# Sliding-window attention beside an MLP: the row maxima reach the q stacks through VectorE's 32x32 squares and transfers, not through a TensorE turn

## The chip, the cores and the metric

One core of a Trainium2 chip runs the whole program. The metric is the device time of one execution in microseconds (us). The kernel before takes 813.5 us (median of 3 runs, 813.16 to 815.95). TensorE (PE) multiplies, PEld is its loading of weights, VectorE is DVE, ScalarE is ACT, GpSimd is POOL, and SyncE (SP) issues every transfer.

## The reference, cut to what matters

```python
qkv = (x @ wqkv) -> q, k, v          # S = 2048 tokens, D = 512, H = 32 heads of 16
scores = q . k * 16 ** -0.5          # masked: 0 <= query - key < 256
p = softmax(scores)                  # over the keys
a = (p . v) @ wo
b = gelu(x @ w1 + b1) @ w2 + b2      # F = 1792
g = sigmoid(sum(x * gate_w))
out = g * a + (1 - g) * b
```

Everything is float32. The softmax is taken with the row maximum subtracted, so the maximum of each query's row has to be known before its exponentials.

## The kernel before, in words

Each dense product is made of three TensorE products of float32r halves (`mm3`, L100 to L103). The projections come first; then the attention and the MLP run interleaved, and the output projection (`final`) ends the program.

Attention goes through 8 groups of 4 heads, and in each group through 16 blocks of 128 tokens. A **step** `u` is one block of keys of one group; there are 128. In a step `att_exp` (L425) makes four score tiles `st` [128 keys x up to 384 queries] (L433), one for each head `i`; ACT takes their exponentials (L445), POOL cuts the edges of the window (L437, L440), and `att_pv` multiplies by v (L465). The exponentials need the maxima of the queries, and these are made by a second pass, `att_max` (L381): for the query block `LEAD` = 6 steps ahead, four tiles `sm` (L389) of the same scores, now with queries on the partitions, and DVE reduces each to its maximum (`M`, L394).

The maximum then has to lie along the columns of the query operand. The stack `qs` holds q for the four heads as 96 rows (high and low parts), and rows 96 and up are for the maxima; `ks` has ones (`own`) in the rows that belong to a head, so that the product `st` comes out with the maximum subtracted. All maxima are handled in **pairs** of blocks (`RB` = 2), 64 pairs in all. `att_rows` (L401) makes the negated maximum as a high and a low part on DVE (`nm`, L405 and L406; 16 columns: 2 blocks, 4 heads, 2 parts). `att_turn` (L410) turns it on TensorE with a product by the identity (L413, tile `mp` in the same three PSUM buffers as `sm`), and ACT writes the rows into `qs` twice (L418), once for each block of the pair, with a scale of 0 or 1 from `odd` that clears the rows of the other block. A pair's rows are first read by `st` two steps after the step that made the last of its maxima has ended.

A chunk of 4 blocks of q and k comes from DRAM for each next group (`att_load`, L353 and L354, every fourth step, when the max block's number leaves `LPOS` = 2 after division by 4); v comes in `att_load_v` (L376); the sums of a chunk go out (`ND`, L477) and are divided in `att_norm` (L500 to L512).

The order on PE, ACT, DVE and POOL is written out by the program: a clock of modelled nanoseconds (`tick`) advances with the products, and work is put in with `after(ns, ...)` when it falls due. Each step takes `STEP` = 2345 ns of dense work from the MLP (3150 ns, `STEP0`, in the first `LEAD` steps, which only make maxima). The order on SP is made by the scheduler from the dependencies. Each transfer has one of eight semaphores in turn, and waits until the transfer eight before it has landed.

Of the kernel before, what the change touches and what calls it, by code (L numbers as in the profile page):

```python
# [32 lines left out]
def gated_mix(ctx: ExitStack, tc: tile.TileContext, x, wqkv, wo, w1, b1, w2, b2, gate_w, out):  # L33
    nc = tc.nc
    x = x[0]
    out = out[0]

    cp = ctx.enter_context(tc.tile_pool(name="cp", bufs=1))
    sb = ctx.enter_context(tc.tile_pool(name="sb", bufs=1))
    dr = ctx.enter_context(tc.tile_pool(name="dr", bufs=1, space=DRAM))  # L40
    ps = ctx.enter_context(tc.tile_pool(name="ps", bufs=1, space=PSUM))
# [3 lines left out]
    def f32(ap):  # L45
        return ap.bitcast(F32)
# [16 lines left out]
    identr = cp.tile([128, 128], F32R, name="identr")  # L63
# [10 lines left out]
                            compare_op=ALU.is_ge, fill=NEG, base=-1, channel_multiplier=-1)  # L74
    nc.gpsimd.affine_select(out=mask[:, 256:384], in_=mask[:, 256:384], pattern=[[-1, 128]],
                            compare_op=ALU.is_ge, fill=NEG, base=0, channel_multiplier=1)


    own = cp.tile([128, 4], F32, name="own")
    nil = cp.tile([128, 1], F32, name="nil")  # L80
    nc.gpsimd.memset(nil, 0.0)
    nc.gpsimd.memset(own, 0.0)
    for k in (0, 1, 8, 9):
        nc.gpsimd.affine_select(out=own[96:112], in_=own[96:112], pattern=[[-2, 4]], compare_op=ALU.not_equal,
                                fill=1.0, base=-k, channel_multiplier=1)
    odd = cp.tile([128, 2], F32, name="odd")
    nc.gpsimd.memset(odd, 0.0)
    nc.gpsimd.memset(odd[96:104, 0:1], 1.0)
    nc.gpsimd.affine_select(out=odd[96:112, 1:2], in_=odd[96:112, 1:2], pattern=[[0, 1]], compare_op=ALU.is_ge,
                            fill=1.0, base=7, channel_multiplier=-1)  # L90
    nms = [cp.tile([128, 112], F32R, name=f"nm{i}") for i in range(2)]
    for nm in nms:
        nc.gpsimd.memset(f32(nm), 0.0)
    vbuf = cp.tile([128, 2, NB * 68 + 16], F32, name="vbuf")
# [83 lines left out]
    qs = cp.tile([128, 2, S], F32R, name="qs")  # L178
# [221 lines left out]
    def att_rows(g_, rb):  # L400

        need(*[("max", g_, rb * RB + b, i) for b in range(RB) for i in range(4)])
        m = Ms.pop((g_, rb))
        nm = nms[rb % 2][:, 96:112].rearrange("p (b i k) -> p k b i", b=RB, k=2)
        nc.vector.tensor_scalar(nm[:, 0], m, -1.0, None, op0=ALU.mult)  # L405
        nc.vector.scalar_tensor_tensor(nm[:, 1], m, -1.0, f32(nm[:, 0]), op0=ALU.mult, op1=ALU.subtract)  # L406
        done.add(("nm", g_, rb))

    def att_turn(g_, rb):

        need(("nm", g_, rb))
        p = ps.tile([112, 128], F32, tag="sm", bufs=3, name=f"mp{g_}_{rb}")
        nc.tensor.matmul(p, nms[rb % 2], identr, start=True, stop=True)  # L413

        def put():
            for b in range(RB):
                cols = slice((rb * RB + b) * 128, (rb * RB + b + 1) * 128)
                nc.scalar.activation(qs[96:112, :, cols], p[96:112].unsqueeze(1).broadcast_to([16, 2, 128]),  # L418
                    AF.Copy, scale=odd[96:112, b:b + 1])
            done.add(("rows", g_, rb))  # L420
        tick(67)
        after(100, put)

    def att_exp(g_, kb, i):

        pr, s = divmod(i, 2)
        w = min(384, S - kb * 128)
        if s == 0:
            pts[g_, kb, pr] = sb.tile([128, 2, 384], F32, tag="pt", bufs=11, name=f"pt{g_}_{kb}_{pr}")
        pt = pts[g_, kb, pr]  # L430
        need(*[("rows", g_, b) for b in range(kb // RB, (kb + w // 128 - 1) // RB + 1)])
        p = ps.tile([128, 384], F32, tag="st", bufs=2, name=f"st{g_}_{kb}_{i}")
        nc.tensor.matmul(p[:, :w], ks[:, pr, s, kb * 128:(kb + 1) * 128],  # L433
                         qs[:, pr, kb * 128:kb * 128 + w], start=True, stop=True)

        def sel():
            nc.gpsimd.affine_select(out=pt[:, :, 0:128], in_=pt[:, :, 0:128], pattern=[[0, 2], [1, 128]],  # L437
                                    compare_op=ALU.is_ge, fill=0.0, base=0, channel_multiplier=-1)
            if w == 384:
                nc.gpsimd.affine_select(out=pt[:, :, 256:384], in_=pt[:, :, 256:384], pattern=[[0, 2], [-1, 128]],  # L440
                                        compare_op=ALU.is_ge, fill=0.0, base=-1, channel_multiplier=1)
            done.add(("pt", g_, kb, pr))

        def exp():
            nc.scalar.activation(pt[:, s, :w], p[:, :w], AF.Exp, scale=SCALE)  # L445
            if s == 1:
                after(500, sel)
        tick(w / 2.4 + 13)
        after(100, exp)
# [257 lines left out]
    turn = None  # L707
    for u in range(-LEAD, NU):
        m = u + LEAD
        gm, bm = divmod(m, NKB)  # L710
        step = STEP if u >= 0 else STEP0
        for i in range(4):
            for op in ORDER:
                if op == "s" and u >= 0:
                    att_exp(u // NKB, u % NKB, i)
                if op == "m" and m < NU:
                    att_max(gm, bm, i ^ XOR)
                if op == "p" and i == PVAT and u >= 1:
                    att_pvs(u - 1)
                if op == "p" and i == PVAT and turn:  # L720
                    att_turn(*turn)
                    turn = None
                if op == "f":
                    fill(step / 4 / ORDER.count("f"))
        if m < NU and bm % RB == RB - 1:
            after(900, att_rows, gm, bm // RB)
            turn = (gm, bm // RB)
# [9 lines left out]

MANUAL = {mybir.EngineType.PE, mybir.EngineType.Activation, mybir.EngineType.DVE, mybir.EngineType.Pool}
MM3 = 3 * 227
LPOS = 2  # L740
LASTN = 2
YLAND = 3200
WARM = (7, 3)
RB = 2
NKB = S // 128
LEAD = 6
START = 117e3
NORM = 6000
GELU = (700, 1500, 2300, 3300, 4200, 5000)
# [5 lines left out]
AHEAD = 11e3  # L755
STEP0 = 3150.0
PVAT = 2
STEP = 2345.0
_TC = dict()
_INS = ["A_x", "A_wqkv", "A_wo", "B_w1", "B_b1", "B_w2", "B_b2", "gate_w"]  # L760

# [17 lines left out]
```

## Time and profile before

| | |
|---|---|
| median of 3 runs | 813.5 us |
| profiled execution, its time | 813.36 us |
| profiled execution, its span | 811.4 us |
| DVE busy | 513.7 us (63%) |
| ACT busy | 483.4 us (60%) |
| POOL busy | 338.7 us (42%) |
| L413, the turn, on PE: 64 | 19.8 us, mean 310 ns |
| L418, the rows written by ACT: 128 | 53.0 us, mean 460 ns |

The span runs from the first to the last instruction. Matmuls are pipelined, so the busy time of one overlaps that of the next: what a matmul takes from the engine is the time from its start to the next one's start, in the timeline, and not its own duration. An engine's idle time before an instruction is listed with what ended it. On SP only the issue of a transfer is seen, not its landing; a landing shows where something waits for it.

### The profile page before, as it was taken

The numbers are of one execution on the slowest core, as the hardware profiler recorded it, in microseconds if no ns is written. First come the engines' busy times: TensorE is split into PE (matmuls) and PEld (weight loads), VectorE is DVE, ScalarE is ACT, GpSimd is POOL, SyncE is SP. The second block draws the span as 40 slices with busy tenths as digits, with TensorE's granted clock in tenths as the row PEclk, the third lists the DMA queues.
The fourth block names the chain that finished last, engine by engine and source line by source line (L and its number), as shares of the span: only waits on it lengthen the run. The fifth ranks groups of instructions, "written<-read, shape, count | busy, mean of one in ns | idle before, by whom it ended". The sixth has DMA issues, their size and how long they took to land.

```text
span 811.4 us, 14841 instructions
## 1 busy us (share of the span) xinstructions
PE 788.5 (97%) x4694; PEld 616.6 (76%) x4694; DVE 513.7 (63%) x1517; ACT 483.4 (60%) x993; POOL 338.7 (42%) x611
## 2 busy tenths in 40 slices
PE   8999999999999999999999999999999999999998
PEld 6788888867877777688767867877777778777767
DVE  5433332887478758856885688568757865784353
ACT  4434423587568557755875677567656764876631
POOL 3200002396336425542784386336524552574100
PEclk9999999999999999999999999999999999999999
DMA  8985856536542734443234555542664363335873
GB/s 260 387 308 195 304 174 211 195 89 215 164 137 66 227 116 119 122 156 104 86 101 132 171 156 173 152 143 86 192 179 129 99 202 113 97 118 186 249 260 117
DMA packets 94925, 135.72 MB, mean 167 GB/s; under 512 B 32256, under 2 KB 43776, under 8 KB 94848
## 3 DMA queue, kind: packets, MB, share of 16 engines
q1 hardware_dynamic: 94848, 134.79, 52.3%
q8 instruction: 37, 0.61, 0.3%
q14 instruction: 40, 0.33, 0.1%
HBM read 79.70 MB, written 55.05 MB: 166 GB/s over the span
## 4 chain that ended last, share of the span: by engine, by line
PE 78%; DVE 8%; ACT 7%; DMA 2%; issue 2%; SPq 1%; POOL 1%; POOLq 0%; DVEq 0%; ACTq 0%
PE st L433 9%; PE pv L465 9%; PE sm L389 8%; PE y L101 6%; PE y L103 6%; PE y L102 6%; PE u L101 4%; PE u L102 4%; PE u L103 4%; PE qk L101 3%; PE qk L103 3%; PE qk L102 3%; DVE jm L394 2%; ACT pt L445 2%; PE v L103 2%
## 5 line engine op out<-in xcount | busy, mean ns | idle before, releaser
L394 DVE CUSTOM_DVE_ANT_0 jm<-sm,mask 128x384 bf16<-128x384 f32 (+2 forms) x512 | 270.6, 528 | 150.1 <-PE sm L389 128.7
L445 ACT ACTIVATE pt<-st 128x384 f32<-128x384 f32 (+2 forms) x512 | 231.0, 471 | 120.6 <-PE st L433 102.9
L437 POOL TENSOR_SCALAR_AFFINE_SELECT pt<-pt 128x256 f32<-128x256 f32 x256 | 122.3, 478 | 248.8 <-ACT pt L445 248.2
L433 PE MATMUL st<-qs,ks 128*128 128x384 f32 (+2 forms) x512 | 172.1, 338 | 8.1 <-ACT pt L445 7.1
L389 PE MATMUL sm<-ks,qs 96*128 96x384 f32 (+2 forms) x512 | 169.6, 332 | 1.8 <-DVE M L394 0.8
L433 PEld LDWEIGHTS st<-qs,ks 128*128 128x128 f32 x512 | 97.0, 190 | 37.1 <-ACT pt L445 19.4
L389 PEld LDWEIGHTS sm<-ks,qs 96*128 96x128 f32 x512 | 96.2, 188 | 26.0 <-DVE M L394 5.2
L440 POOL TENSOR_SCALAR_AFFINE_SELECT pt<-pt 128x256 f32<-128x256 f32 x224 | 101.9, 455 | 0.0
L465 PE MATMUL pv<-pt,vbuf 128*32 128x384 f32 (+2 forms) x1408 | 91.6, 389 | 0.1
L101 PE MATMUL y<-w,h 128*128 128x512 f32 x224 | 89.4, 399 | 0.0
L103 PE MATMUL y<-w,h 128*128 128x512 f32 x224 | 87.7, 391 | 1.3 <-POOL h L574 1.3
L102 PE MATMUL y<-w,h 128*128 128x512 f32 x224 | 87.7, 391 | 0.0
L574 POOL TENSOR_TENSOR h<-x1h,h 128x512 fp32r<-128x512 f32 x56 | 72.5, 1294 | 35.6 <-DVE h L571 35.2
L101 PE MATMUL u<-mx,w 128*128 128x512 f32 x196 | 79.3, 404 | 0.0
L102 PE MATMUL u<-mx,w 128*128 128x512 f32 x196 | 76.7, 391 | 0.0
L103 PE MATMUL u<-mx,w 128*128 128x512 f32 x196 | 76.6, 391 | 0.0
L418 ACT ACTIVATE qs<-mp,odd 16x256 fp32r<-16x256 f32 x128 | 53.0, 460 | 38.9 <-PE mp L413 37.9
L465 PEld LDWEIGHTS pv<-pt,vbuf 128*32 128x32 f32 x1408 | 38.5, 109 | 37.2 <-issue 24.2
L562 DVE SCALAR_TENSOR_TENSOR sqh<-sqh,x1h 128x512 f32<-128x512 f32 x56 | 51.6, 921 | 13.2 <-ACT sqh L559 13.2
L565 ACT ACTIVATE sqh<-sqh 128x512 f32<-128x512 f32 x56 | 35.5, 634 | 36.8 <-DVE sqh L562 36.2
L160 POOL TENSOR_TENSOR w<-raw_w,w 128x512 fp32r<-128x512 f32 x28 | 38.4, 1370 | 40.3 <-ACT w L156 40.2
L256 DVE TENSOR_TENSOR qke<-qk,qke 128x512 fp32r<-128x512 f32 x32 | 22.1, 691 | 51.3 <-ACT qke L253 49.6
(122 smaller groups left out, 1247.7 us busy)
## 6 DMA issues: line engine op xcount, KB each, us to landing
mx<-XT SPq DMA_DIRECT2D x24, 512.0 KB
SQ<-qke SPq DMA_DIRECT2D x16, 512.0 KB
SK<-qke SPq DMA_DIRECT2D x16, 512.0 KB
qs<-SQ SPq DMA_DIRECT2D x64, 128.0 KB
ND<-nd SPq DMA_DIRECT2D x32, 256.0 KB
ks<-SK SPq DMA_DIRECT2D x60, 128.0 KB
raw_w<-in_B_w_dram SPq DMA_DIRECT2D x28, 256.0 KB
SV<-vx SPq DMA_DIRECT2D x16, 272.0 KB
```

What stands on the lines that cost most here:

```text
L101: nc.tensor.matmul(p, lh, rh, start=first, stop=False)
L102: nc.tensor.matmul(p, lh, rl, start=False, stop=False)
L103: nc.tensor.matmul(p, ll, rh, start=False, stop=last)
L389: nc.tensor.matmul(p[:, :w], qs[0:96, pr, b * 128:(b + 1) * 128], ks[0:96, pr, s, k0:k0 + w], start=True, stop=True)
L394: nc.vector.tensor_tensor_reduce(junk[:, :w], p[:, :w], mask[:, 384 - w:384], 1.0, -3e38, ALU.add, ALU.max, M[:, b % RB, i:i + 1])
L418: nc.scalar.activation(qs[96:112, :, cols], p[96:112].unsqueeze(1).broadcast_to([16, 2, 128]), AF.Copy, scale=odd[96:112, b:b + 1])
L433: nc.tensor.matmul(p[:, :w], ks[:, pr, s, kb * 128:(kb + 1) * 128], qs[:, pr, kb * 128:kb * 128 + w], start=True, stop=True)
L437: nc.gpsimd.affine_select(out=pt[:, :, 0:128], in_=pt[:, :, 0:128], pattern=[[0, 2], [1, 128]], compare_op=ALU.is_ge, fill=0.0, base=0, ch ...
L440: nc.gpsimd.affine_select(out=pt[:, :, 256:384], in_=pt[:, :, 256:384], pattern=[[0, 2], [-1, 128]], compare_op=ALU.is_ge, fill=0.0, base= ...
L445: nc.scalar.activation(pt[:, s, :w], p[:, :w], AF.Exp, scale=SCALE)
L465: nc.tensor.matmul(pv[32 * i:32 * i + 32, q - c * T:e - c * T], vt[:, 68 * (kb % NB) + 17 * i:68 * (kb % NB) + 17 * i + 32], pts[g_, kb, i ...
L574: nc.gpsimd.tensor_sub(h[:, 1], x1, f32(h[:, 0]))
```

## The change

The negated maxima are kept as 32 columns per block, of which 8 are used (4 heads, 2 parts). DVE transposes the 128 x 64 tile in squares of 32 x 32 into `tt`: the square of tokens 32 i to 32 i + 31 then has its 8 rows on the partitions 32 i to 32 i + 7. Eight transfers (for the two halves of `qs` and the four squares: 8 rows, 2 blocks, 32 columns, 2 KB each) put them into rows 96 to 103 of `qs`. Each query block now has rows of its own, so `odd` is gone, and `own` is set for 8 rows. `att_turn`, its product and its two ACT instructions are gone. The maxima run seven blocks ahead (`LEAD` 7), the loads stay at the same step of the exponentials (`LPOS` 3), and `STEP` goes from 2345 to 2320 ns.

```diff
-    for k in (0, 1, 8, 9):
-        nc.gpsimd.affine_select(out=own[96:112], ...)
-    odd = cp.tile([128, 2], F32, name="odd")
...
-    nms = [cp.tile([128, 112], F32R, name=f"nm{i}") for i in range(2)]
+    for k in (0, 1):
+        nc.gpsimd.affine_select(out=own[96:104], ...)
+    nms = [cp.tile([128, RB, 32], F32R, name=f"nm{i}") for i in range(2)]
...
-        nm = nms[rb % 2][:, 96:112].rearrange("p (b i k) -> p k b i", b=RB, k=2)
+        nm = nms[rb % 2][:, :, 0:8].rearrange("p b (i k) -> p k b i", k=2)
         nc.vector.tensor_scalar(nm[:, 0], m, -1.0, None, op0=ALU.mult)
         nc.vector.scalar_tensor_tensor(nm[:, 1], m, -1.0, f32(nm[:, 0]), op0=ALU.mult, op1=ALU.subtract)
-        done.add(("nm", g_, rb))
-
-    def att_turn(g_, rb):
-
-        need(("nm", g_, rb))
-        p = ps.tile([112, 128], F32, tag="sm", bufs=3, name=f"mp{g_}_{rb}")
-        nc.tensor.matmul(p, nms[rb % 2], identr, start=True, stop=True)
+
+        tt = sb.tile([128, RB, 32], F32, tag="tt", bufs=2, name=f"tt{g_}_{rb}")
+        nc.vector.transpose(tt.rearrange("p b c -> p (b c)"), f32(nms[rb % 2]).rearrange("p b c -> p (b c)"))
 
         def put():
-            for b in range(RB):
-                cols = slice((rb * RB + b) * 128, (rb * RB + b + 1) * 128)
-                nc.scalar.activation(qs[96:112, :, cols], p[96:112].unsqueeze(1).broadcast_to([16, 2, 128]),
-                    AF.Copy, scale=odd[96:112, b:b + 1])
+            for pr in range(2):
+                for i in range(4):
+                    dst = f32(qs[96:104, pr, rb * RB * 128:(rb + 1) * RB * 128])
+                    dst = dst.rearrange("r (b i j) -> r b i j", b=RB, i=4)[:, :, i]
+                    nc.sync.dma_start(dst, tt[32 * i:32 * i + 8])
             done.add(("rows", g_, rb))
-        tick(67)
-        after(100, put)
+        after(PUT, put)
...
-LPOS = 2
+LPOS = 3
+PUT = 800
-LEAD = 6
+LEAD = 7
-STEP = 2345.0
+STEP = 2320.0
```

On PE the turn stood between the products with v and the next dense product. Before (`st`, `sm` with group-block-head numbers, `y` a product of the MLP):

```order
L465 MATMUL pv_2_4238<-pt_8_1_4124,vbuf 32x384 x2
L465 MATMUL pv_2_4238<-pt_9_0_4167,vbuf 32x384 x2
L465 MATMUL pv_2_4238<-pt_9_1_4190,vbuf 32x384 x2
L413 MATMUL mp_7_4258<-identr,nm_171 112x128
L101 MATMUL y_02_4260<-w_0_1503,h_0_3521 128x512
L102 MATMUL y_02_4260<-w_0_1503,h_0_3521 128x512
L103 MATMUL y_02_4260<-w_0_1503,h_0_3521 128x512
L389 MATMUL sm_0_2_4269<-ks,qs 128x128
```

The same place of the change:

```order
L455 MATMUL pv_2_4403<-pt_8_1_4279,vbuf 32x384 x2
L455 MATMUL pv_2_4403<-pt_9_0_4316,vbuf 32x384 x2
L455 MATMUL pv_2_4403<-pt_9_1_4354,vbuf 32x384 x2
L95 MATMUL y_02_4358<-w_3_1717,h_3_3829 128x512
L96 MATMUL y_02_4358<-w_3_1717,h_3_3829 128x512
L97 MATMUL y_02_4358<-w_3_1717,h_3_3829 128x512
L383 MATMUL sm_1_2_4426<-ks,qs 128x256
L423 MATMUL st_10_3_4429<-qs,ks 128x384
```

And the same step from its start, with the semaphores that each instruction waits for (DMAHW0 to 7 are those of the transfers):

```order
L383 MATMUL sm_1_1_4378<-ks,qs 128x256 [waits DVE_49]
L423 MATMUL st_10_0_4382<-qs,ks 128x384 [waits DMAHW3_49,DMAHW2_49,DMAHW4_49,DMAHW1_49,Activation_49]
L95 MATMUL y_02_4358<-w_2_1649,h_2_3753 128x512
L96 MATMUL y_02_4358<-w_2_1649,h_2_3753 128x512
L97 MATMUL y_02_4358<-w_2_1649,h_2_3753 128x512
L383 MATMUL sm_1_0_4389<-ks,qs 128x256 [waits DVE_49]
L423 MATMUL st_10_1_4392<-qs,ks 128x384 [waits Activation_49]
L383 MATMUL sm_1_3_4395<-ks,qs 128x256 [waits DVE_49]
L423 MATMUL st_10_2_4400<-qs,ks 128x384 [waits DMAHW6_49,DMAHW5_49,DMAHW7_49,DMAHW0_49,Activation_49]
```

The `mp` row is gone, the maxima made beside `st` of block 10 are now those of block 1 of the next group, where they were those of block 0, and two of the four `st` tiles of an even block wait for four transfers each.

On SP, at a place where the MLP loads its next x, the transfers after the q loads. Before (`mx` is 4 x 512 KB of x for the MLP, `den` and `num` belong to the division, `vbuf` is v):

```order
L353 DMA qs<-SQ_70 32x2x512
L354 DMA qs<-SQ_70 16x2x512
L522 DMA mx_2925<-XT_83 128x1024 x4
L500 DMA den_0_2939<-ND_0_90 128x1x32
L503 DMA num_0_2942<-ND_0_90 128x1x512
L376 DMA vbuf<-SV_80 128x4x68
L353 DMA ks<-SK_75 32x2x512
L507 DMA RD_0_106<-rec_0_2940 128x32
```

The same place of the change:

```order
L347 DMA qs<-SQ_70 32x2x512
L348 DMA qs<-SQ_70 16x2x512
L512 DMA mx_2975<-XT_83 128x1024 x4
L410 DMA qs<-tt_5_2990 8x2x32 x8
L490 DMA den_0_3058<-ND_0_90 128x1x32
L493 DMA num_0_3061<-ND_0_90 128x1x512
L370 DMA vbuf<-SV_80 128x4x68
L611 DMA YA_122<-yo_00_3121 128x512
L497 DMA RD_0_106<-rec_0_3059 128x32
L410 DMA qs<-tt_6_3126 8x2x32 x4
L498 DMA rb_0_3062<-RD_0_106 128x1x512
```

Eight transfers of 2 KB now follow the q loads (one pair of blocks) and eight more come after `vbuf` (the next pair), here with the last four behind `rb`, which waits for the landing of `RD`. SP issues 1160 transfers where it issued 648.

On DVE the transpose follows the two instructions that make `nm`:

```order
L388 ISA M_0_2184 128x1
L399 TENSOR_SCALAR nm_159<-M_14_2062 128x2x4
L400 SCALAR_TENSOR_TENSOR nm_159<-M_14_2062,nm_159 128x2x4 [waits DVE_49]
L403 STREAM_TRANSPOSE tt_7_2198<-nm_159 128x64 [waits DMAHW3_49,DMAHW5_49,DMAHW2_49,DMAHW6_49,DMAHW1_49,DMAHW7_49,DMAHW0_49,DVE_49]
L388 ISA jm_0_0_2202,M_0_2184<-sm_0_0_2200,mask 128x128 [waits PE_49]
```

It is one instruction more per pair; the transfers it waits for are those that read the same buffer of `tt` two pairs earlier.

More of the change, by code (lines that the diff above doesn't have):

```diff
@@ L82, in gated_mix @@
     nc.gpsimd.memset(own, 0.0)
-    for k in (0, 1, 8, 9):
-        nc.gpsimd.affine_select(out=own[96:112], in_=own[96:112], pattern=[[-2, 4]], compare_op=ALU.not_equal,
+    for k in (0, 1):
+        nc.gpsimd.affine_select(out=own[96:104], in_=own[96:104], pattern=[[-2, 4]], compare_op=ALU.not_equal,
                                 fill=1.0, base=-k, channel_multiplier=1)
-    odd = cp.tile([128, 2], F32, name="odd")
[L87 to L90, printed above, removed]
-    nms = [cp.tile([128, 112], F32R, name=f"nm{i}") for i in range(2)]
+    nms = [cp.tile([128, RB, 32], F32R, name=f"nm{i}") for i in range(2)]
     for nm in nms:
@@ L706, in gated_mix @@
     fill(AHEAD)
-    turn = None
     for u in range(-LEAD, NU):
@@ L719, in gated_mix @@
                     att_pvs(u - 1)
-                if op == "p" and i == PVAT and turn:
-                    att_turn(*turn)
-                    turn = None
                 if op == "f":
@@ L726, in gated_mix @@
             after(900, att_rows, gm, bm // RB)
-            turn = (gm, bm // RB)
         if m % NB == LPOS and chunks:
```

## The prediction

> **What bounds the kernel now.** I read the page's first two parts, then the groups, then PE's busy time over the attention, then PE's own waits, of which the second fence picks the seven that touch the change (total, times, longest).
>
> ```profile
> span 811.4 us, 14841 instructions
> ...
> PE 788.5 (97%) x4694; PEld 616.6 (76%) x4694; DVE 513.7 (63%) x1517; ACT 483.4 (60%) x993; POOL 338.7 (42%) x611
> ...
> GB/s 260 387 308 195 304 174 211 195 89 215 164 137 66 227 116 119 122 156 104 86 101 132 171 156 173 152 143 86 192 179 129 99 202 113 97 118 186 249 260 117
> ```
> ```profile
> 140.00:760.00 620.00, 606.52 (x3858) 469.66 (x3860) 441.63 (x1374) 412.41 (x874) 320.38 (x563) 1.00 0.47 143
> ```
>
> PE is busy 97% of the span. The last row is the stretch from 140 to 760 us (busy time and instructions of PE, PEld, DVE, ACT, POOL, then the granted clock, 1.00): of 620 us PE is idle 13.5, so the attention with its interleaved MLP is paced by PE, and the time changes by what leaves PE's sequence, or by new waits in it.
>
> ```profile
> PE mp L413 <- DVE nm L406: 2.1, 2, 1.3
> PE sm L389 <- ACT qs L418: 0.8, 2, 0.5
> PEld sm L389 <- ACT qs L418: 2.7, 5, 0.9
> PE st L433 <- ACT pt L445: 7.1, 15, 1.1
> PEld st L433 <- ACT pt L445: 19.4, 39, 1.4
> PE sm L389 <- DVE M L394: 0.8, 3, 0.4
> PEld sm L389 <- DVE M L394: 5.2, 13, 0.9
> ```
>
> The first three exist only because of the turn; the next two are score tiles that wait for ACT's exponentials; the last two are maxima tiles that wait for DVE to empty a buffer. A wait of PEld can lie partly under a running matmul, so these totals are upper bounds of what PE loses.
>
> **The turn's slots on PE (gone).** One turn in the timeline (start, duration):
>
> ```profile
> 254.70 0.86 PE L465 MATMUL pv<-pt,vbuf 128*32 128x256 f32 x16
> 255.48 0.31 PE L413 MATMUL mp<-identr,nm 128*112 128x128 f32 x1
> 255.63 0.44 PE L101 MATMUL u<-mx,w 128*128 128x512 f32 x1
> ```
>
> The product itself lasts 0.31 us, but the next one starts 0.15 us after it (255.63 - 255.48). A pipelined engine loses the start-to-start time, so 64 turns give 64 x 0.15 = 9.6 us. The upper bound is the whole duration, 64 x 0.31 = 19.8 us; I take 9.6 because the matmul after it shows the overlap. The turn's own wait for `nm` adds 2.1 us.
>
> **What ACT gets back (gone: 128 instructions).** Their group, and the timeline behind the same turn:
>
> ```profile
> L418 ACT ACTIVATE qs<-mp,odd 16x256 fp32r<-16x256 f32 x128 | 53.0, 460 | 38.9 <-PE mp L413 37.9
> ```
> ```profile
> 256.98 0.83 ACT L418 ACTIVATE qs<-mp,odd 16x256 fp32r<-16x256 f32 x2
> 257.86 0.19 PEld L389 LDWEIGHTS sm<-ks,qs 96*128 96x128 f32 x1 [0.31 <-ACT qs L418]
> 258.37 0.19 PEld L433 LDWEIGHTS st<-qs,ks 128*128 128x128 f32 x1 [0.33 <-ACT pt L445]
> ```
>
> The two instructions of a pair hold ACT for 0.83 us, first `sm` waits for its buffer (0.31) and then `st` for an exponential queued behind them (0.33). The waits of `sm` on `qs` go entirely: 2.7 + 0.8 = 3.5 us. Of the 26.5 us in which `st` waits for exponentials a part goes. L418 is 53.0 of ACT's 412.4 us there (13%), but as a block of 0.83 it delays more than its share; I take a fifth, 5.3 us, with bounds 0 and 26.5. Together the gains are 9.6 + 2.1 + 3.5 + 5.3 = 20.5 us.
>
> **What DVE gets (added: 64 transposes of 128x64).** The two instructions that make `nm` (least, median and longest ns), and the pair of the same turn in the timeline, with the step's first `st` and POOL beside it:
>
> ```profile
> L405 DVE TENSOR_SCALAR nm<-M x64: 158/210/1157, 142.2 to 738.0; 128x8 fp32r<-128x8 f32 x64
> L406 DVE SCALAR_TENSOR_TENSOR nm<-M,nm x64: 167/171/1279, 142.4 to 738.2; 128x8 fp32r<-128x8 f32 x64
> ```
> ```profile
> 252.37 0.34 PE L433 MATMUL st<-qs,ks 128*128 128x384 f32 x1
> ...
> 253.06 1.29 POOL L574 TENSOR_TENSOR h<-x1h,h 128x512 fp32r<-128x512 f32 x1
> 253.31 1.06 DVE L405 TENSOR_SCALAR nm<-M 128x8 fp32r<-128x8 f32 x1
> 254.41 0.41 DVE L406 SCALAR_TENSOR_TENSOR nm<-M,nm 128x8 fp32r<-128x8 f32 x1
> ```
>
> No row shows a transpose. The nearest are these two, its neighbours in the chain: 0.17 us at the median of the cheaper, over 1.1 us at worst. I take 0.35 us, above both medians since it moves 64 columns and not 8: 22 us of DVE time, of which 441.6 of 620 are used now. The work lies beside PE; it costs PE only where `sm` waits for DVE, 6.0 us now. Against it, the turn no longer holds one of the three `sm` buffers. I take +3 us, half as much again, with bounds -1 and +12 (three times the present wait). The slow L405 spans just the POOL subtraction of 253.06. The Trainium skill's "SBUF — State Buffer" (section "Who interferes with whom") says DVE and GpSimd lock a shared port pair for a whole instruction, and names `tensor_scalar` among the operations that take it, the transpose not; the trace agrees for L405. If the transpose did take it, each could stand as long as that L405, and DVE would get 64 x 1.06 = 68 us, as in the first rival, which is priced below from rows alone.
>
> **The rows' new way (added: 512 transfers on SP).** The score tiles from first to last, the issue times of two shapes, and SP's queue from the next step on:
>
> ```profile
> L433 PE MATMUL st<-qs,ks x512: 221/339/447, 157.1 to 759.8; 128*128 128x384 f32 x149, 128*128 128x256 f32 x11, 128*128 128x128 f32 x11
> ```
> ```profile
> L354 SPq DMA_DIRECT2D qs<-SQ x64: 302/426/1218, 115.6 to 694.6; - x64
> L500 SPq DMA_DIRECT2D den<-ND x16: 599/600/723, 263.4 to 771.2; - x16
> ```
> ```profile
> 256.95 0.34 PE L433 MATMUL st<-qs,ks 128*128 128x384 f32 x1
> 256.98 0.34 SPq L477 DMA_DIRECT2D ND<-nd  x1
> 257.38 0.42 SPq L353 DMA_DIRECT2D qs<-SQ  x1
> ...
> 258.78 0.43 SPq L354 DMA_DIRECT2D qs<-SQ  x1
> 261.62 1.77 SPq L522 DMA_DIRECT2D mx<-XT  x4
> ...
> 270.95 0.32 SPq L507 DMA_DIRECT2D RD<-rec  x1
> ...
> 273.72 0.60 SPq L508 DMA_DIRECT2D rb<-RD  x1
> ```
>
> A step lasts (759.8 - 157.1) / 511 x 4 = 4.72 us. A pair's rows were due two steps, 9.4 us, after its last maxima's step; with `LEAD` 7 it is three, 14.2 us, and this margin has to hold the new way. In the trace the step after a pair begins with the `st` at 252.37 and `nm` is done at 254.82: 2.5 us. Then come the transpose, 0.35; eight issues of 0.42 (L354, the nearest shape: 16 rows in two pieces; bounds 0.30 and 0.60, its own least and L500), 3.4; and a landing. `rb` waits for the landing of `RD` and is issued 2.8 us after `RD` was, so a small transfer lands in at most that. The sum is 9.1 of 14.2 us on a free SP.
>
> Ahead of every second set stand `ND` and the q loads, which end at 259.2, 2.3 us after the `st` that begins the step (256.95), while the transpose is done at 2.5 + 0.35: they cost the set nothing. The worst is a set behind the four `mx` (24 of them, so six times): their issue adds 1.8, and 4 x 512 KB at the best slice's 387 GB/s take 5.4 us. The set's last four also wait for the semaphores of these transfers: issued by 2.3 + 1.8 + 5.4 + 4 x 0.42 = 11.2, they land by 14.0, with half a step more to go since only the third tile reads them. Just in time. I take +2 us for late rows and for the transfers behind them (`rb`, YA, `raw_w`), bounds 0 and the second rival.
>
> SP itself: in four steps, 18.9 us, it issues eight q and k loads, `ND` and `vbuf` (10 x 0.42 = 4.2), and up to 4.0 more (`mx` 1.77, `den` and `rb` 0.60 each, `RD` 0.32, two stores like `ND`). Two sets add 16 x 0.42 = 6.7: 14.9 of 18.9 us. It would be full at (18.9 - 8.2) / 16 = 0.67 us each, above L500's 0.60.
>
> **Moved at no cost.** The dense work in the steps is 128 x 2345 + 6 x 3150 = 319.06 us of the program's clock, and 128 x 2320 + 7 x 3150 = 319.01 now: the end is not moved. The loads keep their step of `st`, but the maxima reach new columns after five steps instead of six, 23.6 us; with the sets ahead of them a load is late by 3.4. The four semaphores on `st` have a row beside them:
>
> ```profile
> L389 PE MATMUL sm<-ks,qs 96*128 96x384 f32 (+2 forms) x512 | 169.6, 332 | 1.8 <-DVE M L394 0.8 <-ACT qs L418 0.8
> ```
>
> The first `sm` of a chunk waits on loads too, and no transfer ended any idle time there: nothing, unless the rows are late.
>
> **The sum.** Against the profiled execution's 813.36 us: -20.5 + 3 + 2 = -15.5, so 797.9. The median of the runs lies 0.1 above it: **798.0 us**. Its own range: half of the exponentials' wait and no costs, -9.6 - 2.1 - 3.5 - 13.2 = -28 at the low end, reached only if all goes well, so 789; only the slots and `nm` with DVE at +6 and +2 late, 810 at the high end.
>
> **The rivals.**
>
> *DVE takes over the wait.* `nm` and the transpose stand behind POOL in a row, `sm` waits three times as much (+12), and the exponentials gain nothing: 813.5 - 15.2 + 12 = 810. For it: DVE is at 71% and one L405 took 1.06 us. Against: a pair is 9.4 us and DVE idles 178 of 620.
>
> *The turn's time was not PE's to give:* the 0.15 us slots come back as waits elsewhere, 812. For it: `st` waits already on ACT. Against: ACT loses 53 us as well, and POOL is at 52%.
>
> *SP delivers late (the slower side).* In-order issue and eight semaphores: a set behind a transfer that waits for its producer, or behind big loads, lands after 14.2 us, and PE stands. The place is the first and third `st` of each even block. From 0.24 us of lateness per pair (15.5 / 64) it eats the whole gain; at 0.5 us more per pair than I allow, 64 x 0.5 = 32 us, it is 830. For it: the six `mx` sets have no margin, `rb` stands in the middle of some sets. Against: 5 us of margin elsewhere, SP at 79%.
>
> *Each transfer pays its landing alone:* 8 x 2.8 = 22.4 us per pair beside 4.1 of other issues, against 9.4 for two steps: 64 x 17 = 1100 us more, some 1900. Against: the q loads start 0.47 us apart in the trace, and none waits for the one before. The Trainium skill's "DMA: Bandwidth & Descriptors" (section "Rules for kernel authors") says under 64 KB a transfer is mostly overhead and many should be one; the rows agree on the price of a landing, not that it adds up.
>
> **Numbers.** Chances: forecast 0.78, DVE 0.08, no gain 0.03, SP late 0.10, landings alone 0.01. A measurement here can tell some 0.5% (4 us) from no change: under 809.4 is faster, over 817.6 slower. The second and third cases lie between: faster 0.78, same 0.11, slower 0.11. The range, 789 to 811, holds the forecast's own and the first rival, and leaves out the others, under 2 in 10.
>
> **What would show it.** In the changed profile: no `mp` and no L418, ACT near 430 us, PE some 20 us less busy; 64 transposes near 0.35 us; transfer issues near 0.42 us; no wait of `st` on `qs<-tt` beyond a few us in all, those behind `mx`; `sm` waiting for DVE under 10 us. I am wrong if `st` waits for transfers by tens of us, if an issue costs over 0.6 us, if a transpose costs over 1 us, or if PE's idle grows by what the slots gave.

## The result, and the profile after

The changed kernel takes 887.48 us at the median, the kernel before 813.33 on the same chip: a ratio of 1.0907, 95% interval 1.0886 to 1.0927. It is **slower by 74 us**; 798 had been forecast. The profiled execution takes 888.05 us. One of the six executions of the changed kernel took 1528.33 us, far from the others (885.27 to 889.34); it is left out, and no trace shows what it did.

First the page of the changed kernel: span, busy times, the granted clock in 40 slices, the chain of waits by engine and by line, and the groups of the two products of a step.

```profile
span 886.0 us, 15485 instructions
...
PE 810.0 (91%) x4630; PEld 624.8 (71%) x4630; DVE 528.7 (60%) x1581; ACT 428.3 (48%) x865; POOL 336.9 (38%) x606
...
PEclk9999999999999999999989899999988999999989
...
PE 59%; DMA 13%; SPq 12%; DVE 7%; issue 4%; ACT 3%; POOL 2%; DVEq 0%; POOLq 0%; ACTq 0%
SPq L410 8%; PE st L423 6%; PE pv L455 6%; PE sm L383 6%; PE y L95 4%; PE y L96 4%; PE y L97 4%; PE u L95 4%; PE qk L95 3%; PE qk L97 3%; PE qk L96 3%; DVE jm L388 3%; PE u L96 3%; PE u L97 3%; DMA den<-ND 3%
...
L383 PE MATMUL sm<-ks,qs 96*128 96x384 f32 (+2 forms) x512 | 175.8, 344 | 48.0 <-DVE M L388 44.5
L423 PE MATMUL st<-qs,ks 128*128 128x384 f32 (+2 forms) x512 | 175.6, 345 | 14.7 <-DMA qs<-tt 7.3
```

PE's idle time went from 22.9 us (811.4 - 788.5) to 76.0. The costliest line of the chain is L410, the transfers that the change adds, and it stands there under SP's queue (SPq). The products that read the rows (`st`) waited only 7.3 us for them; it is `sm`, a product that reads no row, that stood 44.5 us, and for DVE. The weight load (PEld) and the product of one tile can stand in the same stall, so the two rows of a tile are not added up. The waits of the changed kernel show what DVE stood for (total, times, longest):

```profile
PEld sm L383 <- DVE M L388: 61.2, 37, 6.9
DVE rec L496 <- DMA den<-ND: 54.9, 13, 8.3
PE sm L383 <- DVE M L388: 44.5, 18, 6.5
...
PEld st L423 <- ACT pt L435: 16.5, 33, 2.0
DVE yo L610 <- DMA YB<-yo: 16.2, 7, 10.4
...
PE st L423 <- DMA qs<-tt: 7.3, 5, 3.5
```

Before, DVE stood once for `den`, and SP stood most for its producers. In the kernel before:

```profile
DVE rec L506 <- DMA den<-ND: 0.2, 1, 0.2
```
```profile
SPq L477 <- ACT nd L476: 96.8, 29, 9.9
```

In the changed kernel SP's longest total is another line's:

```profile
SPq L251 <- DVE qke L250: 28.4, 15, 2.8
```

SP hardly waits at the sums (L467 now, 3.4 us), since they are done when it gets to them. Its issues, each run of like ones taken as one block, fill 604 of the 670 us from 150 to 820 (90%); in the kernel before they fill 212 of the 600 from 150 to 750 (35%). The two new instructions of the change (count, then least, median and longest ns):

```profile
L410 SPq DMA_DIRECT2D qs<-tt x512: 674/685/1431, 142.4 to 809.1; - x171
L403 DVE STREAM_TRANSPOSE tt<-nm x64: 245/245/248, 142.1 to 802.4; 128x64 f32<-128x64 f32 x64
```

The transpose is cheaper than the 0.35 us of the forecast, the issue dearer than its 0.42. One stall in the timeline of the changed kernel, in order of time (start, duration; idle time and its releaser in brackets):

```profile
301.12 5.83 SPq L410 DMA_DIRECT2D qs<-tt  x8
...
304.65 0.25 DVE L403 STREAM_TRANSPOSE tt<-nm 128x64 f32<-128x64 f32 x1
...
305.91 0.39 PE L97 MATMUL y<-w,h 128*128 128x512 f32 x1
307.00 0.60 SPq L490 DMA_DIRECT2D den<-ND  x1
...
309.06 0.35 DVE L496 RECIPROCAL rec<-den 128x32 f32<-128x32 f32 x1 [4.16 <-DMA den<-ND]
...
309.89 0.52 PE L383 MATMUL sm<-ks,qs 96*128 96x384 f32 x1 [3.58 <-DVE M L388]
```

The eight transfers of a pair hold SP for 5.83 us, 0.73 from one to the next; `den` is issued right behind them. DVE executes in order, reaches the reciprocal and stands 4.16 us; the maxima behind it are not taken, no `sm` buffer comes free, and PE stops. Then one thing more (stretch, length, busy time of PE, PEld, DVE, ACT, POOL, granted clock, DMA share, GB/s):

```profile
307.00:310.00 3.00, 0.11 (x1) 0.12 (x1) 0.80 (x4) 0.00 (x0) 0.04 (x1) 1.00 0.35 57
310.20:313.40 3.20, 3.20 (x10) 2.72 (x10) 2.03 (x8) 0.98 (x2) 0.08 (x1) 0.50 0.75 237
```

After the stall, in which PE stood 3.58 us, TensorE runs at half its clock: through the whole second stretch, and in shorter ones from 310.1 to 313.5, some 3.4 us. Over the span the mean clock is 0.969, against 1.000 before: (1 - 0.969) x 886 = 27 us, if the products are held back in proportion (an estimate), over a third of the loss. The Trainium skill ("TensorE: Matmul & The Clock Gate", section "Part 1: The HAM clock gate") says that the clock falls to half after an idle window of about 3.4 us and comes back after a busy one as long; the trace agrees, with a stall of 3.58 us and 3.4 us at half speed.

### The profile page after: what moved, and what is told of

It reads as the page before. It is cut to its first block, busy times and chain, and to the rows that moved or that the text cites. A ratio compares the mean times of both kernels' runs of the same rounds, so it can differ in the third digit from the quotient of the medians.

```text
span 886.0 us, 15485 instructions
## 1 busy us (share of the span) xinstructions
PE 810.0 (91%) x4630; PEld 624.8 (71%) x4630; DVE 528.7 (60%) x1581; ACT 428.3 (48%) x865; POOL 336.9 (38%) x606
## 4 chain that ended last, share of the span: by engine, by line
PE 59%; DMA 13%; SPq 12%; DVE 7%; issue 4%; ACT 3%; POOL 2%; DVEq 0%; POOLq 0%; ACTq 0%
SPq L410 8%; PE st L423 6%; PE pv L455 6%; PE sm L383 6%; PE y L95 4%; PE y L96 4%; PE y L97 4%; PE u L95 4%; PE qk L95 3%; PE qk L97 3%; PE qk L96 3%; DVE jm L388 3%; PE u L96 3%; PE u L97 3%; DMA den<-ND 3%
## 5 line engine op out<-in xcount | busy, mean ns | idle before, releaser
L383 PE MATMUL sm<-ks,qs 96*128 96x384 f32 (+2 forms) x512 | 175.8, 344 | 48.0 <-DVE M L388 44.5
L423 PE MATMUL st<-qs,ks 128*128 128x384 f32 (+2 forms) x512 | 175.6, 345 | 14.7 <-DMA qs<-tt 7.3
L383 PEld LDWEIGHTS sm<-ks,qs 96*128 96x128 f32 x512 | 99.0, 193 | 83.0 <-DVE M L388 61.2
L423 PEld LDWEIGHTS st<-qs,ks 128*128 128x128 f32 x512 | 99.6, 195 | 44.1 <-ACT pt L435 16.5
L455 PE MATMUL pv<-pt,vbuf 128*32 128x384 f32 (+2 forms) x1408 | 95.6, 399 | 0.7 <-POOL pt L427 0.5
L95 PE MATMUL y<-w,h 128*128 128x512 f32 x224 | 92.9, 415 | 0.1
L97 PE MATMUL y<-w,h 128*128 128x512 f32 x224 | 89.2, 398 | 0.6 <-POOL h L564 0.6
L96 PE MATMUL y<-w,h 128*128 128x512 f32 x224 | 89.5, 400 | 0.0
L95 PE MATMUL u<-mx,w 128*128 128x512 f32 x196 | 82.3, 420 | 0.0
L96 PE MATMUL u<-mx,w 128*128 128x512 f32 x196 | 78.4, 400 | 0.0
L97 PE MATMUL u<-mx,w 128*128 128x512 f32 x196 | 78.1, 398 | 0.0
L95 PEld LDWEIGHTS y<-w,h 128*128 128x128 f32 x224 | 43.4, 194 | 12.5 <-issue 11.2
```

The costliest lines, as they stand in the source:

```text
L95: nc.tensor.matmul(p, lh, rh, start=first, stop=False)
L96: nc.tensor.matmul(p, lh, rl, start=False, stop=False)
L97: nc.tensor.matmul(p, ll, rh, start=False, stop=last)
L383: nc.tensor.matmul(p[:, :w], qs[0:96, pr, b * 128:(b + 1) * 128], ks[0:96, pr, s, k0:k0 + w], start=True, stop=True)
L455: nc.tensor.matmul(pv[32 * i:32 * i + 32, q - c * T:e - c * T], vt[:, 68 * (kb % NB) + 17 * i:68 * (kb % NB) + 17 * i + 32], pts[g_, kb, i ...
```

## The experiments

The first theory (**A**): SP has more to issue than time; transfers other than the rows come late, DVE stands for them in its order, and PE for DVE. Its rivals: **B**, the new lead makes the stalls; **C**, the transposes load DVE; **D**, `st` waits for rows. Later A is split: **A1**, SP's throughput is the bound wherever the lateness shows; **A2**, only DVE's stand before `den` counts. All ratios are to the kernel before on the same chip.

**The lead alone** (kernel before, turn kept):

```diff
-LPOS = 2
-LEAD = 6
-STEP = 2345.0
+LPOS = 3
+LEAD = 7
+STEP = 2320.0
```

> The kernel before with the numbers of the change alone (LEAD 7, LPOS 3, STEP 2320); the turn stays on TensorE and no transfer is added. Theory A (SP is full: 512 issues of 0.73 us start to start push every other transfer back, DVE stands in its own order for late den, ya and YB, and PE for DVE) expects 810 to 816 us, and SP as idle as before. Theory B (the new lead or the smaller dense share of a step makes the stalls) expects over 850 us.

832.24 us, ratio 1.0238 (1.0221 to 1.0254): a miss. Its waits:

```profile
PEld mp L413 <- DVE nm L406: 23.0, 27, 2.4
PE mp L413 <- DVE nm L406: 14.1, 17, 2.1
```

They stand at the turn, which PE waited 2.1 us for before. With an odd lead the program puts the turn in a step with no pv products ahead of it; that DVE has not caught up for this reason is likely, but the run changes `STEP` as well. The changed kernel has no turn, so this does not carry over as it is; but it says that the lead is not free (see the runs without transfers).

**The transposes alone** (kernel before, 64 unread transposes):

```diff
+        tt = sb.tile([128, 64], F32, tag="tt", bufs=2, name=f"tt{g_}_{rb}")
+        nc.vector.transpose(tt, f32(nms[rb % 2])[:, 48:112])
```

> The kernel before with a DVE transpose of 128x64 after each nm, whose result nobody reads: 64 instructions of 0.245 us. Theory A expects 812 to 818 us: DVE has room. Theory C (the DVE work itself makes sm wait) expects a good part of the 74 us, over 840 us.

817.28 us, ratio 1.0065 (1.0043 to 1.0087): some 4 to 5 us for 64 of them, where the forecast had 3 (a freed `sm` buffer set against them). C falls as the cause of 74.

**16 rows to a transfer** (changed kernel; eight of them zeros; the columns of `nm` and the rows of `own` that go with it are not shown):

```diff
-                    dst = f32(qs[96:104, pr, rb * RB * 128:(rb + 1) * RB * 128])
+                    dst = f32(qs[96:112, pr, rb * RB * 128:(rb + 1) * RB * 128])
-                    nc.sync.dma_start(dst, tt[32 * i:32 * i + 8])
+                    nc.sync.dma_start(dst, tt[32 * i:32 * i + 16])
```

> The changed kernel, but each of the 8 transfers of a pair carries 16 rows, zeros among them (the two blocks of a pair on rows of their own, own as before): as many transfers, twice the bytes, on 16 partitions instead of 8. If the issue costs 0.69 us because a transfer has only 8 rows, it falls to 0.42 us, SP to some 75 per cent, and the time to 795 to 808 us (theory A with that cause). If the price is that of 128-byte pieces or of SBUF as the source, the issue stays at 0.69 us or more and the time at 885 to 895 us.

872.32 us, ratio 1.0731 (1.0712 to 1.0751). Its transfers:

```profile
L410 SPq DMA_DIRECT2D qs<-tt x512: 585/592/1817, 141.7 to 793.2; - x171
```

This is neither of the two expected times. Twice the bytes, and 15 us faster, with an issue 0.09 us shorter: the number of bytes and of 128-byte pieces is not what costs. The number of rows is a small part of an issue's price; most of it stays.

**As many transfers that nobody reads** (kernel before, with its turn; eight extra per pair):

```diff
+        away = sb.tile([128, 8, 2, 34], F32, tag="away", bufs=1, name=f"away{g_}_{rb}")
+        def extra():
+            for n in range(8):
+                i = n % 4
+                nc.sync.dma_start(away[96:104, n, :, 0:32],
+                                  f32(nms[rb % 2])[32 * i:32 * i + 8, 48:112].rearrange("r (b j) -> r b j", b=2))
+        after(800, extra)
```

> The kernel before, turn and all, with 8 extra transfers per pair of the change's shape (8 rows, 2 pieces of 32) from nm into a tile that nobody reads. Theory A expects SP full and 870 to 900 us though no product waits for a row. Theory D (the lost time is st waiting for rows that land late) expects under 825 us.

869.12 us in a single run, 1 us under what A expected. Its transfers, and two of its waits:

```profile
L413 SPq DMA_DIRECT2D away<-nm x512: 673/686/1516, 142.7 to 796.8; - x171
```
```profile
DVE rec L514 <- DMA den<-ND: 41.2, 13, 8.1
PEld sm L389 <- DVE M L394: 37.4, 25, 7.0
```

No product reads these, the lead is 6 and the turn is in place, and still 56 us are lost by the same chain. A is shown for most of the loss (56 of 74 us); D and B fall as its main cause.

**DVE's reciprocal later in its order** (changed kernel):

```diff
-        after(NORM, rcp), after(3 * NORM, mul)
+        after(3 * NORM, rcp), after(6 * NORM, mul)
```

> The changed kernel with the division's DVE instructions put later in the order (reciprocal at three NORM instead of one, the product at six instead of three), so that DVE does not stand waiting for den. Theory A1 (SP's own throughput is the bound: 95 per cent busy in every stretch of the attention) expects a gain of under 20 us, 868 to 890 us, since the lateness shows up elsewhere (ya, YB, rows). Theory A2 (SP is late but could catch up; what costs is DVE standing in its own order for den) expects 40 us or more back, under 848 us.

904.49 us, ratio 1.1114 (1.1090 to 1.1137). Both A1 (868 to 890) and A2 (under 848) missed. DVE no longer waits for `den`; others wait instead:

```profile
PEld st L423 <- ACT pt L435: 41.2, 45, 4.0
...
PE st L423 <- DMA qs<-tt: 25.5, 14, 5.2
```

`sm` stands for DVE still, 20.9 us in place of 44.5. A2 falls: the lateness moves to whoever stands next in SP's queue, as A1 says. That the time grows by 17 us, A1 does not say, and no run explains it.

**Half the transfers** (changed kernel; only the first half of `qs` gets rows, so two of four heads go without their maximum):

```diff
-            for pr in range(2):
+            for pr in range(1):
```

> The changed kernel with half of the transfers: the maxima rows go into the first half of qs only, so heads 2 and 3 of each group have no maximum subtracted (that part of the result is left out). SP then has 256 issues of 0.73 us, some 75 per cent. Theory A expects most of the loss gone: 800 to 820 us. If it was the lead and the order rather than SP, it stays over 830 us.

816.04 us, ratio 1.0027 (1.0005 to 1.0049). An issue costs the same (0.686 us), but SP has time to wait for its producers again:

```profile
SPq L410 <- DVE M L388: 77.5, 34, 7.6
```

DVE stands 11.3 us for `den`, where it stood 54.9. The first 256 transfers cost little, the second 256 cost 71 us: a queue that is nearly full, not a price per transfer. But the forecast's gain is not there either.

**The second half issued by ACT** (changed kernel):

```diff
-        after(PUT, put)
+        after(PUT, put, 0, nc.sync), after(3 * PUT, put, 1, nc.scalar)
```

(Only the calls are shown; `put` takes the half and the queue.)

> The changed kernel with the four transfers of the second half of qs issued by ACT instead of SP: all 512 transfers, half of the issue time off SP. If the issue time on SP's queue is what counts, 805 to 835 us, ACT paying some 0.7 us for each of its 256. If the number of small transfers in the DMA engines counts, it stays over 870 us.

955.96 us in a single run, a miss. ACT, which the exponentials need, now has 256 issues of 0.70 us in its own order, and stands there for transfers:

```profile
PEld st L423 <- ACT pt L435: 103.9, 70, 4.3
ACT pt L435 <- DMA qs<-tt: 86.5, 36, 5.7
```

So this run does not tell SP's issues from the number of transfers: it is also over the 870 us that the other answer expected.

**The price of an issue by itself** (transfers alone, no attention; 14 of each shape on SP):

> Transfers alone, 14 of each shape on SP's queue, nothing of the model computed (the output is zeros): the price of an issue. If rows under 16 cost, 8 rows are dearer than 16 in every kind; if pieces of 128 bytes cost, 2 x 32 is dearer than 2 x 512 of the same rows; if SBUF as the source costs, the same shape from DRAM is cheaper. The changed kernel's shape should show its 0.685 us, L354's its 0.426 us.

In the names, r is rows and p pieces, "fr" reads from DRAM and "tor" writes to it; "small" is 32 columns, "long" 512.

```profile
L59 SPq DMA_DIRECT2D r8p2small<-src x14: 673/677/873, 2.4 to 11.9; - x14
```
```profile
L59 SPq DMA_DIRECT2D r16p2small<-src x14: 585/592/642, 14.3 to 22.6; - x14
```
```profile
L59 SPq DMA_DIRECT2D r64p2small<-src x14: 593/606/704, 35.7 to 44.2; - x14
```
```profile
L59 SPq DMA_DIRECT2D fr16p2long<-far x14: 541/568/593, 111.7 to 120.4; - x14
```
```profile
L59 SPq DMA_DIRECT2D tor8p2small<-src x14: 297/298/486, 109.2 to 124.3; - x14
```
```profile
L75 SPq DMA_DIRECT2D out_dram<-src x16: 426/636/652, 124.6 to 134.1; - x16
```

Eight rows cost 0.08 more than 16, and 64 cost about as much as 16. Neither the length of a piece nor where it is read from matters much (16 rows: 0.586 with 512 columns, 0.590 from DRAM); eight rows in one piece instead of two took 0.624. The eight-row store to DRAM costs less than half of the one to SBUF, but the last line, which stores the output (128 rows of 2 KB) to DRAM, costs 0.636. So the place alone does not set the price. The Trainium skill ("DMA: Bandwidth & Descriptors", section "Why a DMA increments its semaphore by 16 and not by 1") says that the sequencer itself writes the part of a completion that unused engines don't; the step between 8 and 16 rows would fit it, though no run shows the mechanism. The 0.42 us of L354 in the kernel is below the 0.568 of its shape here; why stays open.

**Where the forecast's gain is.** Three answers stood against each other: **G1**, the odd lead takes it; **G2**, it never was TensorE's to give; **G3**, what SP still has to issue eats it. The changed kernel without its transfers, at both leads: no maximum reaches `qs`, and none is subtracted. The diff is against the change; the second run keeps `LEAD` 7, `LPOS` 3 and `STEP` 2320:

```diff
-            for pr in range(2):
-                for i in range(4):
...
-                    nc.sync.dma_start(dst, tt[32 * i:32 * i + 8])
-LPOS = 3
-LEAD = 7
-STEP = 2320.0
+LPOS = 2
+LEAD = 6
+STEP = 2345.0
```

> The change without its transfers, and with LEAD, LPOS and STEP of the kernel before (the maxima are not subtracted: that part of the computation is left out; VectorE's negation, remainder and transpose stay). Nothing turns and nothing delivers, so it is the most that taking the turn away can give. The forecast: 813.5 less 20.5 for the turn plus 3 for the transposes, 796. G1 and G3: 794 to 801. G2: 810 to 816.

> The same without transfers, but with the change's LEAD 7, LPOS 3 and STEP 2320. G1, the odd lead: 10 to 20 us above the run with LEAD 6, 808 to 816. G3, SP: as the run with LEAD 6 within 2 us, 794 to 801. G2: 810 to 816, as the run with LEAD 6.

LEAD 6: 802.43 us, ratio 0.9875 (0.9844 to 0.9905). LEAD 7: 808.13, ratio 0.9945 (0.9928 to 0.9961). The first lies between what G1 and G3 expected (794 to 801) and what G2 did (810 to 816). Waits at LEAD 6, then at LEAD 7:

```profile
PEld st L418 <- ACT pt L430: 16.7, 32, 1.3
...
PE st L418 <- ACT pt L430: 6.7, 15, 1.0
PEld sm L383 <- DVE M L388: 4.9, 9, 1.2
...
PE sm L383 <- DVE M L388: 2.1, 3, 0.9
```
```profile
PEld sm L383 <- DVE M L388: 15.2, 22, 2.2
...
PE sm L383 <- DVE M L388: 7.3, 8, 1.9
```

Even with a free delivery, taking the turn away gives 10 us, not 17.5 (20.5 - 3), and the set of `LEAD` 7, `LPOS` 3, `STEP` 2320 gives back 5.7 of them: PE's own wait at `sm` for DVE goes from 2.1 to 7.3 us. That is rival B with its true size. So the set holds 5.7 us (whether it is the odd lead, as G1 says, or `STEP`, these two runs do not tell), G3 the 7 to 8 us from here to the run with half the transfers, and G2, in part, the 7 us by which the 10 fall short of the forecast.

**Four blocks to a set** (256 transfers carry all rows; against the change):

```diff
-RB = 2
-LEAD = 7
+RB = 4
+LEAD = 8
```

> The change with four blocks in a set instead of two and LEAD 8 instead of 7 (three full steps of slack after a set's last maximum become two): 256 transfers of 8 rows by four blocks carry the same 2048 rows. SP's throughput as the bound of the change (A1): SP spends half as long on them, and the time comes down to about that of the change with half its transfers, 816, or below. Where the forecast's gain of 15 us went is asked beside it. G1, the odd lead (the step after the negation holds no pv matmuls, so TensorE comes back to the maxima before VectorE has caught up): with the even lead 795 to 804. G2, the gain never was TensorE's to give: 810 to 816. G3, what SP still has to issue eats it: 812 to 820. Were the bytes or the rows and not the issues the matter, 870 to 890.

> As before with four blocks in a set, but LEAD 10 (chunks of q loaded two steps later against the lead): four steps of slack, and the negation falls ahead of the step with the pv matmuls of four blocks. If rows came late for st at LEAD 8, this one is faster than LEAD 8 by what st waited for; G1: 795 to 804, as LEAD 8 or a little below; G2 and G3: 810 to 820. The start, with ten steps of maxima ahead of the first st instead of seven, may cost up to 5 us in either.

LEAD 8: 847.34 us, ratio 1.0411 (1.0380 to 1.0443). LEAD 10 (with `LPOS` 1, no loads in the first steps): 843.70, ratio 1.0379 (1.0353 to 1.0405). Both missed; the number of issues is not enough of an explanation. At LEAD 8 SP's issues fill 65% of the stretch from 150 to 780 us, in the run with half the transfers 67% of that from 150 to 750, and yet the one loses 35 us and the other 3. At LEAD 8, then at LEAD 10:

```profile
PE st L423 <- DMA qs<-tt: 28.2, 17, 4.7
```
```profile
PE sm L383 <- DMA qs<-SQ: 23.6, 9, 5.7
```

In the first the rows stand behind eight loads of the same step and come late; in the second the loads do. Three runs give them room: loads a step behind the rows (`LPOS` 0, first chunk skipped), then 16 rows to a transfer, then LEAD 9.

> Four blocks to a set, LEAD 8, but the loads of keys and queries issued one step after the rows instead of just ahead of them (LPOS 0; three steps until they are read). If the 847 was the order on SP's queue, the waits of st for rows (28 us) and what they cost in clock go: 808 to 818, about the run without transfers at the forecast's lead (802) plus the 8 that 256 transfers cost in the half run. If the rows of four blocks are late whatever stands ahead of them, or if the count of pieces or bytes counts, 835 to 850.

> The same with 16 rows to a transfer (eight of them zeros), which in the run of the change with 16 rows made an issue 0.09 us shorter: SP's time on the rows falls by 24 us of 175. If what SP issues is still the price at 256 transfers, 2 to 5 us below the 8-row run; if nothing of SP's time is on the path any more, the same within 1.5 us. Below 809 it would beat the kernel before.

> As the run with 16 rows, LEAD 9: three steps of slack for the rows and three for the loads, but an odd lead, so that the negation falls in a step ahead of one without pv matmuls. If lateness still costs at LEAD 8, this one is faster by 3 to 10 us; if the parity of the lead counts (802 against 808 in the runs without transfers), slower by 2 to 6.

836.49 us, ratio 1.0273 (1.0231 to 1.0314); 828.31, ratio 1.0204 (1.0174 to 1.0235); 818.60, ratio 1.0080 (1.0050 to 1.0110). `st` in the first still waits for rows:

```profile
PE st L423 <- DMA qs<-tt: 9.7, 7, 4.5
```

The first missed its 808 to 818: moving the loads recovers 11 us, not 30. Shorter issues recover 8 by the medians and 6 by the ratios (2 to 5 were expected; the two intervals overlap), and a step more of room another 10, though its lead is odd. So the place in SP's order and the room count beside the number of issues. That a burst of eight needs more of both than one of four is likely, not shown: four blocks to a set without transfers, which would price the rest of that change, was not run.

**Delivery without SP** (against the change; LEAD 6, `LPOS` 2, `STEP` 2345, `PUT` 300; four copies per pair from the squares' partitions to the stacks', on ACT, POOL or DVE; POOL's, cut):

```diff
-                    nc.sync.dma_start(dst, tt[32 * i:32 * i + 8])
+                src = tt[32 * i:32 * i + 8].unsqueeze(1).broadcast_to([8, 2, RB, 32])
+                nc.gpsimd.tensor_copy(dst, src)
```

> The change at LEAD 6, LPOS 2, STEP 2345, its eight transfers for two blocks replaced by four ScalarE copies (8 rows by 2 pairs by 2 blocks by 32 columns each); SP issues none of the rows. The kernel before had two copies of 0.46 us there; four of about 0.33 (a half of the elements) make ScalarE some 30 us busier than before. If SP is the whole price of the squares: 802 to 808, 5 to 10 below the kernel before, the first version under it with a full result. If the squares' way itself costs (rows later, order of VectorE): 812 to 820.

> The same with the four copies on GpSimd, 38% busy in the change. If SP is the whole price: 802 to 812, the upper end if a copy there takes over 0.6 us and the selects of pt behind it come late for the pv matmuls. If the way itself costs: 812 to 825.

> The same with the four copies on VectorE right behind its transpose, some 0.2 us each, 50 us in all on the engine whose maxima sm waits for. If SP is the whole price: 803 to 812, about 0.1 us of sm's wait for each of 64 sets above the run without transfers or more. If the way itself costs: 812 to 825.

ACT 833.04 us, ratio 1.0236 (1.0211 to 1.0262); POOL 813.63, ratio 1.0014 (0.9993 to 1.0034); DVE 838.82, ratio 1.0322 (1.0295 to 1.0350). On ACT, on POOL (its copies, then two waits), on DVE:

```profile
ACT qs L410 <- DVE tt L403: 66.8, 62, 2.3
PEld st L423 <- ACT pt L435: 45.2, 62, 1.8
```
```profile
L410 POOL CAST qs<-tt x256: 284/289/755, 142.8 to 739.4; 8x128 fp32r<-8x128 f32 x128
```
```profile
PE y L97 <- POOL h L564: 3.6, 2, 2.4
PE pv L455 <- POOL pt L430: 3.3, 4, 2.0
```
```profile
PEld sm L383 <- DVE M L388: 26.5, 39, 2.5
```

All three are above what was expected if SP were the whole price (802 to 812 at most), so the delivery costs without SP too; ACT and DVE are above the other range as well (820 and 825). POOL can nearly afford it: the changed kernel's loss is gone, and the time is that of the kernel before, but 11 us above the run with no delivery. Its copies add 96 us to POOL, and PE then stands 6.9 us for POOL (`y` and `pv`), where it stood 1.7 in that run. The ACT run does not price ACT's copies alone: they were put into its order too early, ACT stands 67 us for the transpose, and the exponentials with it. POOL stands 57 us in the same way; a later place was not tried on either. On DVE the copies delay the maxima. Of the versions with a full result none beats the kernel before.

## Why the prediction was wrong

What the runs add up to, each at its median (on three chips, where the kernel before took 812.7 to 813.3):

| kernel | us | step |
|---|---|---|
| before | 813 | |
| no turn, transposes, no delivery, LEAD 6 | 802.4 | -10 |
| the same, LEAD 7 | 808.1 | +6 |
| half the transfers | 816.0 | +8 |
| all transfers | 887.5 | +71 |

**The step that failed** is "eight issues of 0.42 (L354, the nearest shape ...; bounds 0.30 and 0.60)". An issue measured 0.685 us, 0.73 from start to start, outside both bounds. The prediction's own ledger had SP full at 0.67: with 16 x 0.73 = 11.7 beside up to 8.2 of other work, SP owes up to 19.9 us in every 18.9. "79%" becomes over 100% where all the other work falls together, and in the trace, whose steps have got longer, 90% over the whole attention. The +2 us for late rows and what stands behind them became about 79 (8 + 71). The source was taken by the number of rows and pieces, 16 in two; by price the nearest rows were those of `den` and `rb` at 0.60, used only as the far bound. As this price decides whether the queue is full, the ledger should have been worked out at its upper bound and beyond: 0.60 was already within 11% of the limit.

**The rival "SP delivers late"** had the right engine and the wrong place. It put the price on the first and third `st` of even blocks, and they waited 7.3 us in all. What came late were other transfers on the queue, `den` above all, and the price came by DVE's order, where the maxima stand behind the reciprocal. So it was not 0.5 us per pair (830) but stalls of up to 6.5 us. The prediction had named those behind the rows only as part of its 2 us. It also left out the clock, which fell to half behind such a stall: by the estimate above some 27 of the 74 us.

**The gains** were mis-sized. 20.5 less 3 was forecast; 10 came at LEAD 6. The prediction called the totals of PE and PEld upper bounds, and then added them: 3.5 us for `sm` on `qs`, a fifth of 26.5 for the exponentials. But the two can be one stall (the stall shown above stands as 3.58 us in PE's rows and again as 4.01 in PEld's). By PE's own rows 0.8 was there to gain at `sm`; the exponentials' wait fell only from 7.1 to 6.7; and `sm` waits 1.3 more for DVE. With the slots and `nm` that is 9.6 + 2.1 + 0.8 + 0.4 - 1.3 = 11.6 us, an estimate in which PEld's waits do not count, near the 10 measured. The transposes cost 4 to 5 when added to the kernel before, and the profiled run's clock is 0.996, some 3 us; a remainder of a few us is not told apart. "Moved at no cost" failed for the lead: 5.7 us.

**Right**: L418 and its load on ACT are gone (428 us busy, near 430 was said); the transposes are cheap, 0.245 us; `st` waits for rows a few us only; the turn's waits are gone; no transfer pays its landing alone. Of the signs named for being wrong, the issue over 0.6 us and PE's grown idle time came true; and of those for being right two did not: PE was to be some 20 us less busy and is 21.5 more, and `sm` was to wait for DVE under 10 us. The low end of the range, 789, is not what its own sum gives (813.4 - 28.4 = 785); nothing hung on it. The Trainium skill's rule of many small transfers in one ("DMA: Bandwidth & Descriptors", section "Rules for kernel authors") had been set aside because landings don't add up. They don't, but issues on one queue do.

## What to carry to other kernels

Before giving a queue several hundred small transfers, add up its issue times by the start-to-start time of the dearest like row, not of the cheapest, and ask what is left at that price; a queue near full delays every other transfer in it. Then look for who stands in an in-order engine behind such a transfer, as the damage shows there and not at the new transfer's reader. How full it is on average does not say all: with four blocks to a set and SP's issues at 65% of the time, 35 us were still lost. A small move between partitions may be cheaper as a copy on an engine that has room (POOL, 0.29 us) than as a transfer.

## What the runs showed of the hardware that was not expected

- In the run of transfers alone an issue to SBUF took 0.57 to 0.68 us in the rows above, nearly whatever the bytes, and one to DRAM 0.30 or 0.64 (what sets this, and the 0.42 of the q loads in the full kernel, stays open).
- Eight rows are dearer to issue than 16 by 0.08 to 0.09 us, in the kernel (0.685 and 0.592) and alone (0.677 and 0.592).
- TensorE's clock was halved right behind a stall of 3.6 us, for some 3.4 us.
- A copy by POOL, ACT or DVE from one group of 32 partitions to rows 96 to 103 works, at 0.29, 0.31 and 0.22 us for 8 x 128 elements.
